# Tiled kv products with a compact mask, and denominators spread over four chunks, in a gated linear-attention and SwiGLU kernel

## Chip, cores, metric

The kernel runs on one core of one Trainium2 chip. The metric is the device time of one execution in microseconds (us); a "span" is the time from the first to the last instruction in a profiled execution. A ratio compares runs of the same rounds alone. Engine names: PE is TensorE, DVE is VectorE, ACT is ScalarE, POOL is GpSimd.

## The reference, cut to what matters

```python
# x: (1, 2048, 512) bf16; 32 heads of 16; F = 1376
pq, pk = phi(q), phi(k)                         # q, k, v from x @ wqkv
kv  = einsum("bhsd,bhse->bhde", pk, v)          # one 16x16 block per head
z   = einsum("bhsd->bhd", pk)
num = einsum("bhqd,bhde->bhqe", pq, kv)
den = einsum("bhqd,bhd->bhq", pq, z)[..., None] + 1e-6
a   = reshape(num / den) @ wo
b   = (silu(x @ w1) * (x @ w3)) @ w2
out = g * a + (1 - g) * b                       # g = sigmoid(x . gate_w)
```

The kernel never forms v. It accumulates XP = x^T pk over all tokens, forms kv from wv and XP once, and folds kv and wo into one matrix W. kv is needed only where row and column belong to the same head, so of each 128x128 product only the 16x16 blocks on its diagonal survive a mask.

## The kernel before

The change touches the passage between the sweep over the keys and the SwiGLU chunks of the first 512 tokens. A "chunk" is 128 of the 1376 hidden features; each has four gate_ps and four up_ps products of 512 columns.

```python
kvT_ps = psX.tile([P, KC, P], FP32, tag="XP0", name="kvT_ps")      # KC = 4, P = 128
for c in range(KC):
    csl = slice(c * P, (c + 1) * P)
    for dc in range(KC):
        nc.tensor.matmul(kvT_ps[:, c, :], lhsT=wv_sb[:, dc, csl], rhs=XP_sb[:, dc, csl],
                         start=(dc == 0), stop=(dc == KC - 1))
nc.vector.tensor_tensor(out=kvT_sb[:], in0=kvT_ps[:],
                        in1=blockmask[:, None, :].to_broadcast([P, KC, P]), op=ALU.mult)
emit_omg(0)                            # om and its reciprocal, 128x4
for fc in range(3):
    if fc == 0:
        emit_ffn(0, fc)
        continue
    emit_den(0, 2 * fc - 2)            # qz on GpSimd, then a reduction on VectorE
    emit_ffn(0, fc, between=lambda: emit_den(0, 2 * fc - 1))
    # ... fc == 1: 16 products W_ps, each 32x32, from kvT_sb[gsl, c, gsl]
    for i in ((2, 3) if fc == 1 else (0, 1)):      # ScalarE: W_ps to W_sb
        nc.scalar.activation(out=W_sb[:, i, :], in_=W_ps[i][:], func=ACT.Copy, scale=2.0)
# ... chunks 3 to 9 without denominators
```

In a chunk (emit_ffn) ScalarE makes th = tanh(gate_ps), VectorE makes gs from th and gate_ps, then whatever "between" holds, then hT from up_ps and gs. gate_ps and up_ps come from a pool of four buffers, so the products of chunk n wait for gs and hT of chunk n-2. Chunks 4 and 6 borrow other buffers (XP0 to XP3). Further names in the lines below: r_ps are the products of the last 96 hidden features and of the gate, and hr their hidden product on GpSimd; qz is the product whose sums over a head are the denominators, and rden their reciprocals, which scale pq; om is the 128x4 factor by whose reciprocal the output is scaled.

## Time and profile before

| | before |
|---|---|
| time, median of 3 | 179.11 us (178.67 to 179.57) |
| span of the profiled run | 176.9 us |
| TensorE busy | 97% |
| VectorE, ScalarE, GpSimd busy | 67%, 37%, 38% |
| last r_ps product to first gate_ps (the kv stage) | 0.977 us |
| lost ahead of gate_ps and up_ps of chunk 3 | 0.38 us |

TensorE sets the time. Its busy share hides small losses, because recorded matmuls overlap (a 512-wide one is recorded as 0.38 us long, and the next starts 0.216 us after it).

### The profile page before, as it was taken

The page shows a single profiled execution, that of the slowest core. Times are in us where ns is not written, and L with a number is a line of the kernel's source. Part 1 is how long each engine was busy: PE and PEld are TensorE (multiplying, and loading weights), DVE is VectorE, ACT ScalarE, POOL GpSimd, SP SyncE. Part 2 cuts the span into 40 slices and gives each one's busy share as a digit, 9 for nine tenths or more (in the row PEclk, how much of TensorE's full clock was granted, in tenths as well). Part 3 has the DMA queues.
Part 4 walks back from the last instruction along what each step waited for, and adds up shares of the span by engine and source line. Part 5 has one row for each costly group of instructions (what it writes and reads, how often), then busy time and mean ns, then how long its engine had stood idle before and what let it go on. Part 6 is the DMA issues. An engine that isn't in the chain of part 4 may idle for free.

```text
span 176.9 us, 2497 instructions
## 1 busy us (share of the span) xinstructions
PE 172.3 (97%) x879; PEld 83.1 (47%) x895; DVE 118.6 (67%) x204; ACT 65.2 (37%) x123; POOL 66.5 (38%) x96
## 2 busy tenths in 40 slices
PE   7999999999999999999999999999999999999994
PEld 3444444474445454444454544444545444444463
DVE  0586858899999737597776375978754669776000
ACT  4524224476333333333243333242433323331222
POOL 6197655789064323272003232820032329100000
PEclk9999999999999999999999999999999999999999
DMA  5999899941004011123000111240002012200012
GB/s 175 229 298 223 247 308 364 352 129 28 9 21 97 7 41 37 37 59 89 0 4 7 38 36 37 60 94 2 0 7 66 12 61 59 65 0 0 30 33 59
DMA packets 30381, 15.14 MB, mean 86 GB/s; under 512 B 20929, under 2 KB 30241, under 8 KB 30369
## 3 DMA queue, kind: packets, MB, share of 16 engines
q1 hardware_dynamic: 29952, 14.67, 30.2%
q10 hardware_dynamic: 416, 0.31, 0.6%
q8 instruction: 7, 0.11, 0.3%
q14 instruction: 6, 0.04, 0.1%
HBM read 8.42 MB, written 2.10 MB: 59 GB/s over the span
## 4 chain that ended last, share of the span: by engine, by line
PE 88%; DVE 5%; POOL 3%; issue 2%; ACT 0%; DVEq 0%; POOLq 0%
PE o_ps L372 19%; PE up_ps L330 18%; PE gate_ps L322 18%; PE o_ps L363 8%; PE q_ps L220 6%; PE XP L207 6%; PE k_ps L187 5%; PE r_ps L244 2%; PE k L187 2%; PE o_ps L367 2%; PE warm L164 2%; POOL pks L197 1%; POOL zt L421 1%; DVE hT L342 1%; DVE phi_m L145 1%
## 5 line engine op out<-in xcount | busy, mean ns | idle before, releaser
L322 PE MATMUL gate_ps<-xT,w_sb 128*128 128x512 bf16 x157 | 40.7, 379 | 0.3
L330 PE MATMUL up_ps<-xT,w_sb 128*128 128x512 bf16 x156 | 40.5, 379 | 0.3 <-DVE hT L342 0.2
L228 POOL TENSOR_TENSOR qz<-pq,z_sb 128x512 f32<-128x512 bf16 x16 | 18.5, 1162 | 57.0 <-DVE pq L148 57.0
L335 ACT ACTIVATE th<-gate_ps 128x512 bf16<-128x512 f32 x40 | 23.9, 598 | 39.6 <-PE gate_ps L322 38.1
L372 PE MATMUL o_ps<-w_sb,hT 128*128 128x512 bf16 (+3 forms) x176 | 37.1, 355 | 0.2
L337 DVE SCALAR_TENSOR_TENSOR gs<-th,gate_ps 128x512 bf16<-128x512 bf16 x40 | 27.3, 682 | 5.4 <-ACT th L335 5.1
L342 DVE TENSOR_TENSOR hT<-up_ps,gs 128x512 bf16<-128x512 f32 x40 | 27.6, 691 | 3.7
L145 DVE TENSOR_SCALAR phi_m<-phi_e 128x512 bf16<-128x512 bf16 x32 | 13.6, 424 | 21.2 <-ACT phi_e L143 21.0
L372 PEld LDWEIGHTS <-hT 128*128 128x128 bf16 x180 | 16.8, 98 | 17.8
L330 PEld LDWEIGHTS <-w_sb 128*128 128x128 bf16 x160 | 15.7, 98 | 19.2 <-issue 0.4
L322 PEld LDWEIGHTS <-w_sb 128*128 128x128 bf16 x160 | 15.5, 98 | 18.7 <-issue 0.4
L297 POOL TENSOR_TENSOR pqn<-pq,rden 128x256 bf16<-128x256 bf16 x32 | 19.0, 626 | 13.8 <-DVE rden L288 13.1
L377 ACT ACTIVATE o_out<-o_ps,omg 128x512 bf16<-128x512 f32 x15 | 10.3, 688 | 28.9 <-PE o_ps L372 26.3
L197 POOL TENSOR_TENSOR pks<-pks,pk_sb 128x512 f32<-128x512 f32 x15 | 17.6, 1174 | 7.3 <-DVE pk_sb L148 6.7
L363 PE MATMUL o_ps<-W_sb,pqT 128*128 128x512 bf16 (+3 forms) x71 | 16.6, 355 | 0.1
L220 PE MATMUL q_ps<-wq_sb,xT 128*128 128x512 bf16 x63 | 16.4, 379 | 0.1
L207 PE MATMUL XP<-pk_sb,x_sb 128*128 128x512 bf16 x62 | 16.2, 379 | 0.1
L231 DVE TENSOR_REDUCE den<-qz 128x32 f32<-128x512 f32 x16 | 10.9, 684 | 7.9 <-POOL qz L228 7.8
L143 ACT ACTIVATE phi_e<-k_ps 128x512 bf16<-128x512 f32 x12 | 7.2, 597 | 14.4 <-PE k_ps L187 13.3
L143 ACT ACTIVATE phi_e<-q_ps 128x512 bf16<-128x512 f32 x16 | 9.6, 597 | 7.8 <-PE q_ps L220 7.8
L187 PE MATMUL k_ps<-wk_sb,xT 128*128 128x512 bf16 x48 | 12.3, 379 | 0.0
L148 DVE SCALAR_TENSOR_TENSOR pq<-q_ps,phi_m 128x512 bf16<-128x512 f32 x16 | 11.1, 691 | 0.5
(60 smaller groups left out, 117.1 us busy)
## 6 DMA issues: line engine op xcount, KB each, us to landing
w_sb<-in_B_w_dram SPq DMA_DIRECT2D x4, 640.0 KB, 7.3
out_dram<-o_out SPq DMA_DIRECT2D x15, 128.0 KB, 1.7
w_sb<-in_B_w_dram SPq DMA_DIRECT2D x1, 1280.0 KB, 12.2
x_sb<-in_A_x_dram SPq DMA_DIRECT2D x2, 512.0 KB, 5.2
x_sb<-in_A_x_dram SPq DMA_DIRECT2D x1, 768.0 KB, 5.1
wq_sb<-in_A_wqkv_dram SPq DMA_DIRECT2D x1, 512.0 KB, 6.4
wv_sb<-in_A_wqkv_dram SPq DMA_DIRECT2D x1, 512.0 KB, 6.4
wo_sb<-in_A_wo_dram SPq DMA_DIRECT2D x1, 512.0 KB, 10.0
```

The source lines that it names most:

```text
L187: nc.tensor.matmul(k_ps[:], lhsT=xT[:, kc, t * P : (t + 1) * P], rhs=wk_sb[:, kc, :], start=(kc == 0), stop=(kc == KC - 1),)
L197: nc.gpsimd.tensor_add(pks[:], pks[:], pk_sb[:, t, :])
L207: nc.tensor.matmul(XP_ps[dc][:], lhsT=x_sb[:, t, dc * P : (dc + 1) * P], rhs=pk_sb[:, t, :], start=(t == 0), stop=(t == NT - 1),)
L220: nc.tensor.matmul(q_ps[:], lhsT=xT[:, kc, ts_tok], rhs=wq_sb[:, kc, :], start=(kc == 0), stop=(kc == KC - 1),)
L297: nc.gpsimd.tensor_tensor(out=pqn[:].rearrange("p (i c e) -> p c i e", i=NG, c=KC)[:, :, :, dsl], in0=st[tb, "pq"][:, tt, :].rearrange("p ...
L322: nc.tensor.matmul(gate_ps[:], lhsT=w1_sb[:, kc, fsl], rhs=xT[:, kc, tok_sl], start=(kc == 0), stop=(kc == KC - 1),)
L330: nc.tensor.matmul(up_ps[:], lhsT=w3_sb[:, kc, fsl], rhs=xT[:, kc, tok_sl], start=(kc == 0), stop=(kc == KC - 1),)
L335: nc.scalar.activation(out=th[:], in_=gate_ps[:], func=ACT.Tanh, scale=0.5)
L337: nc.vector.scalar_tensor_tensor(out=gs[:], in0=th[:], scalar=1.0, in1=gate_ps[:], op0=ALU.add, op1=ALU.mult)
L342: nc.vector.tensor_tensor(out=st[tb, "hT"][:, fc, :], in0=up_ps[:], in1=gs[:], op=ALU.mult)
L363: nc.tensor.matmul(o_ps[:], lhsT=st[tb, "pqT"][:, c, tsl], rhs=W_sb[:, c, a:b], start=(c == 0), stop=False,)
L372: nc.tensor.matmul(o_ps[:], lhsT=st[tb, "hT"][:, fc, tsl], rhs=w2_sb[:, fc, a:b], start=False, stop=(fc == FC - 1),)
```

## The change

It has two parts. The kv products compute only 32x32 diagonal blocks: 64 products of 128x32 with 32 moving columns in four column groups take the place of 16 full ones, and the mask is four times smaller. The four reductions of denominators go one to a chunk into chunks 1 to 4, instead of two each into chunks 1 and 2, and the evictions of W_ps on ScalarE get fixed places between the tanh of those chunks.

```diff
+    diagmask = consts.tile([P, G], FP32, name="diagmask")              # G = 32
+    for i in range(NG):
+        gsl = slice(i * G, (i + 1) * G)
+        nc.gpsimd.tensor_copy(diagmask[gsl, :], blockmask[gsl, gsl])
-    kvT_sb = consts.tile([P, KC, P], BF16, name="kvT_sb")
+    kvT_sb = consts.tile([P, KC, G], BF16, name="kvT_sb")
 ...
-        kvT_ps = psX.tile([P, KC, P], FP32, tag="XP0", name="kvT_ps")
+        kvT_ps = psX.tile([P, KC, G], FP32, tag="XP0", name="kvT_ps")
         for c in range(KC):
-            csl = slice(c * P, (c + 1) * P)
             for dc in range(KC):
-                nc.tensor.matmul(
-                    kvT_ps[:, c, :], lhsT=wv_sb[:, dc, csl], rhs=XP_sb[:, dc, csl],
-                    start=(dc == 0), stop=(dc == KC - 1),
-                )
+                for i in range(NG):
+                    bsl = slice(c * P + i * G, c * P + (i + 1) * G)
+                    nc.tensor.matmul(
+                        kvT_ps[i * G : (i + 1) * G, c, :], lhsT=wv_sb[:, dc, bsl],
+                        rhs=XP_sb[:, dc, bsl], start=(dc == 0), stop=(dc == KC - 1),
+                    )
 ... (mask product on 128x4x32, W_ps from kvT_sb[gsl, c, :])
-        for fc in range(3):
-            ...
-            emit_den(0, 2 * fc - 2)
-            emit_ffn(0, fc, between=lambda: emit_den(0, 2 * fc - 1))
+        emit_ffn(0, 0)
+    with tc.manual_schedule(engines={ENG.DVE, ENG.Activation}):
+        for fc in range(1, TPB + 1):
+            emit_ffn(0, fc, between=lambda: emit_den(0, fc - 1))
+            ... (fc == 1: W_ps as before)
+            for i in {1: (2,), 2: (3, 0), 3: (1,)}.get(fc, ()):
+                emit_W_sb(i)
```

More of the change, by code (lines that the diff above doesn't have):

```diff
@@ L445, with emit_W_sb @@
         )
-        kvT_ps = psX.tile([P, KC, P], FP32, tag="XP0", name="kvT_ps")
+        kvT_ps = psX.tile([P, KC, G], FP32, tag="XP0", name="kvT_ps")
         for c in range(KC):
-            csl = slice(c * P, (c + 1) * P)
             for dc in range(KC):
-                nc.tensor.matmul(
-                    kvT_ps[:, c, :], lhsT=wv_sb[:, dc, csl], rhs=XP_sb[:, dc, csl],
-                    start=(dc == 0), stop=(dc == KC - 1),
-                )
+                for i in range(NG):
[4 more added lines that the diff above has]
+                    )
         nc.vector.tensor_tensor(
             out=kvT_sb[:], in0=kvT_ps[:],
-            in1=blockmask[:, None, :].to_broadcast([P, KC, P]), op=ALU.mult,
+            in1=diagmask[:, None, :].to_broadcast([P, KC, G]), op=ALU.mult,
         )
         emit_omg(0)
-        for fc in range(3):
-            if fc == 0:
-                emit_ffn(0, fc)
-                continue
-            emit_den(0, 2 * fc - 2)
-            emit_ffn(0, fc, between=lambda: emit_den(0, 2 * fc - 1))
+        emit_ffn(0, 0)
+    with tc.manual_schedule(engines={ENG.DVE, ENG.Activation}):
+        W_ps = [psX.tile([P, D], FP32, tag=f"XP{i}", name=f"W_ps{i}") for i in range(NG)]
+        def emit_W_sb(i):
+            nc.scalar.activation(out=W_sb[:, i, :], in_=W_ps[i][:], func=ACT.Copy, scale=2.0)
+        for fc in range(1, TPB + 1):
+            emit_ffn(0, fc, between=lambda: emit_den(0, fc - 1))
             if fc == 1:
-                W_ps = [psX.tile([P, D], FP32, tag=f"XP{i}", name=f"W_ps{i}") for i in range(NG)]
                 for i in range(NG):
@@ L471 @@
                         nc.tensor.matmul(
-                            W_ps[i][c * G : (c + 1) * G, :], lhsT=kvT_sb[gsl, c, gsl],
+                            W_ps[i][c * G : (c + 1) * G, :], lhsT=kvT_sb[gsl, c, :],
                             rhs=wo_sb[gsl, c, :], start=True, stop=True,
                         )
-            for i in ((2, 3) if fc == 1 else (0, 1)):
-                nc.scalar.activation(out=W_sb[:, i, :], in_=W_ps[i][:], func=ACT.Copy, scale=2.0)
-    for fc in range(3, FC):
+            for i in {1: (2,), 2: (3, 0), 3: (1,)}.get(fc, ()):
+                emit_W_sb(i)
+    for fc in range(TPB + 1, FC):
         emit_ffn(0, fc)
```

## The prediction

> **What bounds the kernel now.** I read the page first, for the bound.
>
> ```profile
> PE 172.3 (97%) x879; PEld 83.1 (47%) x895; DVE 118.6 (67%) x204; ACT 65.2 (37%) x123; POOL 66.5 (38%) x96
> ...
> PE 88%; DVE 5%; POOL 3%; issue 2%; ACT 0%; DVEq 0%; POOLq 0%
> ```
>
> TensorE (PE) is busy for 97% of the 176.9 us span and makes up 88% of the chain that ended last. So the change is worth what it takes out of TensorE's stream, or puts into it, and nothing else. The list of waits of TensorE has only two entries, and one of them lies in the stage that the change touches:
>
> ```profile
> PE up_ps L330 <- DVE hT L342: 0.2, 1, 0.2
> ```
>
> A busy TensorE can hide more than that, because the recorded end of a matmul overlaps the next one's start. I therefore read starts, not busy time, in the timeline of TensorE from the kv products (L450) on. Columns: start us, us until the last one's recorded end, engine, line.
>
> ```profile
> 37.04 1.06 PE L450 MATMUL kvT_ps<-XP_sb,wv_sb 128*128 128x128 bf16 x16
> 37.93 1.03 PE L322 MATMUL gate_ps<-xT,w_sb 128*128 128x512 bf16 x4
> ...
> 40.52 1.03 PE L330 MATMUL up_ps<-xT,w_sb 128*128 128x512 bf16 x4
> 41.48 0.43 PE L471 MATMUL W_ps<-wo_sb,kvT_sb 32*32 32x512 bf16 x16
> 41.85 1.04 PE L322 MATMUL gate_ps<-xT,w_sb 128*128 128x512 bf16 x4
> 42.72 1.03 PE L330 MATMUL up_ps<-xT,w_sb 128*128 128x512 bf16 x4
> 43.63 1.02 PE L322 MATMUL gate_ps<-xT,w_sb 128*128 128x512 bf16 x4
> 44.83 1.02 PE L330 MATMUL up_ps<-xT,w_sb 128*128 128x512 bf16 x4 [0.17 <-DVE hT L342]
> 45.69 1.03 PE L322 MATMUL gate_ps<-xT,w_sb 128*128 128x512 bf16 x4
> ```
>
> Where nothing waits, a group of four starts 0.863 us after the one before it (44.83 to 45.69), so one 512-wide matmul takes 0.216. From 42.72 to 43.63 is 0.91, that is 0.05 too much; from 43.63 to 44.83 is 1.20, 0.34 too much. The **loss is 0.39 us**, though the wait shows 0.17. Its cause is seen on VectorE (DVE) and GpSimd (POOL):
>
> ```profile
> 39.21 0.65 DVE L454 TENSOR_TENSOR kvT_sb<-kvT_ps,blockmask 128x512 bf16<-128x512 f32 x1
> 39.78 1.03 DVE L275 TENSOR_SCALAR om<-el 128x4 f32<-128x4 f32 x1
> ...
> 40.94 0.66 DVE L337 SCALAR_TENSOR_TENSOR gs<-th,gate_ps 128x512 bf16<-128x512 bf16 x1
> ...
> 44.09 0.68 DVE L342 TENSOR_TENSOR hT<-up_ps,gs 128x512 bf16<-128x512 f32 x1
> ```
>
> ```profile
> 39.62 4.61 POOL L228 TENSOR_TENSOR qz<-pq,z_sb 128x512 f32<-128x512 bf16 x4
> ```
>
> VectorE runs without a pause here and is late: the first gs waited for nothing but VectorE's own queue (its tanh ended at 39.60). Before it stand the kv mask of 0.65 us, and a 128x4 operation of 1.03 us under a running qz. Then chunks 1 and 2 each put two reductions of denominators beside gs and hT: four operations some 0.60 us apart, 2.4 us, against TensorE's 1.73 us a chunk. So the hT of chunk 1 starts at 44.09, and up_ps of chunk 3, which needs its buffer (four in the pool, two a chunk), starts at 44.83. On ScalarE (ACT) four evictions of W_ps stand together:
>
> ```profile
> 41.93 2.06 ACT L476 ACTIVATE W_sb<-W_ps 128x512 bf16<-128x512 f32 x4 [0.61 <-PE W_ps L471]
> 43.85 0.63 ACT L335 ACTIVATE th<-gate_ps 128x512 bf16<-128x512 f32 x1
> ```
>
> The tanh of chunk 2 starts at 43.85, although its gate_ps was done at 42.89: 0.96 us late. This is hidden today, because VectorE reaches the gs of chunk 2 only at 45.28, but it would show once VectorE is quick.
>
> [...]the 16 W_ps products: they start within 0.05 us, so 0.0034 us apart. [...]No kv-like case, the same tile reloaded again and again, is in this trace; nearest is the 64-wide tail of the last output:
>
> ```profile
> 173.79 0.46 PE L372 MATMUL o_ps<-w_sb,hT 128*128 128x64 bf16 x10
> ```
>
> Taking 0.19 for the last one's own duration (the single L367 matmul of that width shows 0.19), nine steps take 0.27 us: 30 ns for a pair of load and matmul. [...]The matmul before it is this one:
>
> ```profile
> 41.17 0.38 PE L330 MATMUL up_ps<-xT,w_sb 128*128 128x512 bf16 x1
> ```
>
> Its stream ends at 41.17 + 0.22 = 41.39, and W_ps starts at 41.48: 0.09 us. The last W_ps product starts at 41.53 and streams until 41.75, the next gate_ps starts at 41.85: 0.10 us. So one visit to a tiled mode costs **0.19 us**. [...]om (L275) of 128x4 takes 1.03 us under qz, while in its three other executions, later in the span, it takes 0.16 us.
>
> **The change, part by part.** (a) kv products. Removed: 16 matmuls of 128 columns, 0.89 us (37.04 to 37.93). Added: 64 of 32 columns, each with a load of 32 columns, in four column groups; the moving columns fall from 16 x 128 = 2048 to 64 x 32 = 2048 if groups ran one after the other, and to 512 if four run at once. If the four of a round overlap,[...] about 30 ns: 16 x 0.030 = 0.48, plus 0.19 for the mode: 0.67 us, so -0.22 us. This is an estimate, from the tail's pair[...]. If they don't overlap,[...] 2.0 us, +1.1 us. I take the first as likelier (55%), because W_ps shows pairs following at 0.0034 us in distinct tiles, column neighbours among them. With 30% for the second and the rest between, the weighted cost is about +0.2 us.
> (b) The mask: 128x128 instead of 128x512 elements. The rden product of 128x128 (L288) takes 0.28 us, so VectorE gains 0.4 us. It is not at the end of a path itself: kvT_sb is ready at 39.86 today and needed at 41.48. Its side effect: om could start at about 39.42, before qz starts at 39.62, and finish in 0.16 us; then a further 0.9 us of VectorE is saved. That is a race of 40 ns and I give it half.
> (c) Denominators: chunks 1 to 4 carry three VectorE operations each, 3 x 0.60 = 1.80 us against 1.73: a drift of 0.07 a chunk, absorbed. Working it out without the luck of (b): gs(0) stays at 40.9, then in steps of 0.60 hT(0) 41.5, gs(1) 42.1, den(0) 42.7, hT(1) 43.3 to 44.0; up_ps of chunk 3 wants its buffer at 44.5. So the whole **0.39 us** goes. The four qz (1.16 us each, the last done at 44.23) come before their reductions.
> (d) ScalarE in fixed order: tanh, then one, two and one evictions of 0.60 us; gate_ps of chunk 2 is evaluated at about 42.9 instead of 43.85. XP2 and XP3 come free before 45, and chunk 4 wants them at 45.35 without the loss. No time of its own, but it makes (c) safe.
> (e) rden is about 1.5 us later, as the fourth reduction moves from chunk 2 to 4. The first pqT (its products start at 50.22 today, its transfer takes 2.3) is wanted at 57.79: 4 us of slack hide it. The four GpSimd copies for the compact mask fit in its idle 3.95 us before 7.66.
> Sum: -0.39 (c) + 0.2 (a, weighted) = about -0.2 us; with the likelier branch of (a) alone -0.6. I write -0.3: 179.11 - 0.3 = **178.8 us**.
>
> **Rivals.** *Serial column groups*: kv takes 2.0 us, +1.1 - 0.39 = +0.7, 179.8 us. [...]Against it: the 0.0034 us of W_ps. *The sequencer becomes the bound*: 128 instructions instead of 32. The trace shows nothing slower than 30 ns for a pair when short; if 64 pairs cost that each, the result is the serial one again. *The loss moves*: a wait of the same size returns at chunk 4 or 6, where buffers XP0 to XP3 are borrowed, or at the first output block through the later rden; then (c) is worth 0 and the time is 179.1 - 0.2 to 180.2. The slacks in (d) and (e) speak against it.
>
> **Range and chances.** The likelier branch gives 178.5, the serial one 179.8, and the three runs of before spread from 178.67 to 179.57. I set 178.1 to 179.8. All branches lie within 1% while 2% is 3.6 us, so same 0.97, faster 0.02, slower 0.01.
>
> **What would show it.** In the timeline after: from the first kv product to gate_ps of chunk 0, 0.67 us if the groups overlap, 2.0 if not; steps of 0.863 from gate_ps of chunk 2 to chunk 4; no wait on hT; kvT_sb at 0.28 us; om at 0.16 or 1.0 us; tanh of chunk 2 within 0.1 us of its gate_ps. The prediction is wrong if kv takes over 2.2 us, if a gap over 0.3 us opens before chunk 8 or at the first output block, or if the stages that the diff doesn't touch change.

The sum came to -0.39 (c) + 0.2 (a, weighted) = about -0.2 us, to -0.6 with the likelier branch of (a), and -0.3 was written. The time of a product behind the serial branch's 2.0 us was the author's estimate without a measurement (with the tail's 30 ns it would be 64 x 0.030 + 0.19 = 2.1 us). Why a round should take 30 ns was not shown. The matmul "before it" is the one before W_ps; the 0.19 us are the 0.09 and 0.10 read around W_ps. Why om is slow under qz was not shown either; what stands is that it took 1.03 us there and 0.16 elsewhere.

## The result

The changed kernel took 178.26 us (median of 6, 177.97 to 178.57), the kernel before 179.27 us (median of 6, 178.61 to 179.57). The ratio is 0.995 with a 95% interval of 0.9926 to 0.9974. A ratio here is the mean time of one kernel's fast runs over that of the other's in the same rounds, so it is not quite the ratio of the quoted medians.

The page of the kernel after, the same two lines:

```profile
PE 173.1 (98%) x943; PEld 83.3 (47%) x943; DVE 117.6 (67%) x204; ACT 65.4 (37%) x123; POOL 67.1 (38%) x100
...
PE 98%; DVE 0%; issue 0%
```

The chain that ended last is now TensorE almost alone, where VectorE and GpSimd had 8% of it. In TensorE's list of waits the one for hT is gone; only that of the warm-up at the start is left:

```profile
PE warm L168 <- PEq L521: 0.8, 1, 0.8
```

The timeline of TensorE in the kernel after (start us, us to the last recorded end, engine, line):

```profile
35.94 1.50 PE L248 MATMUL r_ps<-wr_sb,xT 128*128 128x193 bf16 x16
37.37 0.66 PE L455 MATMUL kvT_ps<-XP_sb,wv_sb 128*32 128x32 bf16 x64
37.96 1.04 PE L326 MATMUL gate_ps<-xT,w_sb 128*128 128x512 bf16 x4
...
41.89 1.04 PE L326 MATMUL gate_ps<-xT,w_sb 128*128 128x512 bf16 x4
42.76 1.03 PE L334 MATMUL up_ps<-xT,w_sb 128*128 128x512 bf16 x4
43.62 1.03 PE L326 MATMUL gate_ps<-xT,w_sb 128*128 128x512 bf16 x4
44.49 1.03 PE L334 MATMUL up_ps<-xT,w_sb 128*128 128x512 bf16 x4
```

From 42.76 on the groups start 0.86 to 0.87 us apart: the 0.38 us of before are gone. The last r_ps product starts at 37.19, so the kv stage takes 37.96 - 37.19 = 0.77 us, against 0.98.

On VectorE and GpSimd of the kernel after:

```profile
39.44 0.25 DVE L459 TENSOR_TENSOR kvT_sb<-kvT_ps,diagmask 128x128 bf16<-128x128 f32 x1
39.62 0.31 DVE L279 TENSOR_SCALAR om<-el 128x4 f32<-128x4 f32 x1
39.96 0.18 DVE L283 RECIPROCAL omg<-om 128x4 f32<-128x4 f32 x1
40.06 0.66 DVE L341 SCALAR_TENSOR_TENSOR gs<-th,gate_ps 128x512 bf16<-128x512 bf16 x1
...
42.62 0.69 DVE L346 TENSOR_TENSOR hT<-up_ps,gs 128x512 bf16<-128x512 f32 x1
```

```profile
38.85 1.05 POOL L261 TENSOR_TENSOR hr<-upr,gsr 128x192 bf16<-128x192 f32 x2
39.87 4.53 POOL L232 TENSOR_TENSOR qz<-pq,z_sb 128x512 f32<-128x512 bf16 x4
```

The mask takes 0.25 us and om 0.31 instead of 1.03: om now ends at 39.93, 0.02 after the last hr, where it used to end (40.81) 0.02 after the first qz. The hT of chunk 1 starts at 42.62 and ends 1.18 us before up_ps of chunk 3 starts. On ScalarE the tanh of chunk 2 comes right after its gate_ps, between evictions:

```profile
42.03 0.60 ACT L471 ACTIVATE W_sb<-W_ps 128x512 bf16<-128x512 f32 x1 [0.67 <-PE W_ps L479]
42.96 0.60 ACT L339 ACTIVATE th<-gate_ps 128x512 bf16<-128x512 f32 x1 [0.33 <-PE gate_ps L326]
```

**Why spans are not compared directly.** The spans are 176.9 and 176.5 us, 0.3 us apart unrounded (176.85 and 176.53). But the first XP product starts at 8.08 us in one trace and at 8.32 in the other:

```profile
8.08 1.03 PE L207 MATMUL XP<-pk_sb,x_sb 128*128 128x512 bf16 x4
```

```profile
8.32 1.03 PE L211 MATMUL XP<-pk_sb,x_sb 128*128 128x512 bf16 x4
```

From that product to the end it is 168.77 us before and 168.21 after: **0.56 us less**, namely 0.21 in the kv stage and 0.37 to 0.38 from the wait, within 0.03 us. In the traces the first XP product starts anywhere from 7.95 to 9.20 us, while "XP to end" repeats to 0.01 us for the same work. So I judge every experiment by XP to end, and the timed runs only say how much of it survives the scatter of the start.

### The profile page after: what moved, and what is told of

Same layout as the page of the kernel before. It is cut to its first block, busy times and chain, and to the rows that moved or that the text cites. A ratio compares the mean times of both kernels' runs of the same rounds, so it can differ in the third digit from the quotient of the medians.

```text
span 176.5 us, 2613 instructions
## 1 busy us (share of the span) xinstructions
PE 173.1 (98%) x943; PEld 83.3 (47%) x943; DVE 117.6 (67%) x204; ACT 65.4 (37%) x123; POOL 67.1 (38%) x100
## 4 chain that ended last, share of the span: by engine, by line
PE 98%; DVE 0%; issue 0%
PE gate_ps L326 20%; PE o_ps L376 20%; PE up_ps L334 20%; PE o_ps L367 8%; PE XP L211 8%; PE q_ps L224 8%; PE k_ps L191 6%; PE r_ps L248 3%; PE k L191 2%; PE o_ps L371 2%; PE warm L168 2%; PE xTp L181 0%; PE kvT_ps L455 0%; PE W_ps L479 0%; DVE o_last L385 0%
## 5 line engine op out<-in xcount | busy, mean ns | idle before, releaser
L334 PE MATMUL up_ps<-xT,w_sb 128*128 128x512 bf16 x160 | 41.1, 379 | 0.0
```

What stands on the lines that cost most here:

```text
L334: nc.tensor.matmul(up_ps[:], lhsT=w3_sb[:, kc, fsl], rhs=xT[:, kc, tok_sl], start=(kc == 0), stop=(kc == KC - 1),)
```

## The experiments

The four questions: does the time agree with the traces' 0.56 us; which part removes the wait; what is the ScalarE order worth; and what paces the kv stage. "Stage" is from the last r_ps product to the first gate_ps; "lost" is the sum of gaps over the normal step between gate_ps and up_ps groups from chunk 2 on. The single runs had no repetition, so only their traces count.

| run | stage us | lost us | XP to end us | ratio (95%) |
|---|---|---|---|---|
| before | 0.977 | 0.38 | 168.77 | |
| after | 0.770 | 0 | 168.21 | 0.995 (0.9926 to 0.9974) |
| after_again | 0.770 | 0 | 168.21 | 0.9987 (0.9964 to 1.0009) |
| kv_only | 0.772 | 0 | 168.21 | 0.9959 (0.9938 to 0.9981) |
| den_only | 0.976 | 0 | 168.40 | 0.9982 (0.9962 to 1.0001) |
| om_early | 0.977 | 0 | 168.41 | 0.9991 (0.9969 to 1.0013) |
| mask_copies_only | 0.976 | 0.37 | 168.77 | 1.0012 (0.999 to 1.0035) |
| den_only_act_free | 0.977 | 0.27 | 168.68 | single run |
| act_free | 0.771 | 0.26 | 168.47 | single run |
| kv_only_plus2 | 0.770 | 0.90 | 169.11 | single run |
| after_plus2 | 0.771 | 0.28 (0.05 more at chunk 9) | 168.54 | single run |
| groups_serial | 0.874 | 0 | 168.32 | single run |
| kv_twice | 1.305 | 0 | 168.82 | single run |
| one_group_extra | 2.355 | 0 | 169.80 | single run |

### The whole change again (after_again)

No edit.

> The whole change again, for a narrower interval, because the first measurement (178.26 against 179.27 us, 1.0 us less) gave more than the two traces show: from the first XP product to the end 168.22 us against 168.77, that is 0.56 us less (kv stage 0.21, the wait for hT 0.39, small change elsewhere). If only the stage counts, the ratio comes out near 1 - 0.56/179.2 = 0.9969, so about 178.6 us beside 179.2. If something at the start of the program changes too, the ratio stays at 0.995, and XP starts earlier than in the kernel before.

Measured: 178.76 us (median of 6) beside 179.12 (median of 11). XP to end is again 168.21 us. The interval of the first rounds (0.9926 to 0.9974) and of these (0.9964 to 1.0009) both hold 0.9969, which is 1 - 0.56/179.2. So the 1.0 us of the first medians was in part luck, and the traces' 0.56 us is the size that all results agree with. Of the start: XP began at 8.79 us here, later than before, so nothing in the start got faster.

### The kv part alone (kv_only)

```diff
 (kernel before, plus: diagmask, the 64 tiled products, the 128x4x32 mask)
 (denominators and ScalarE order as before)
```

> Only the tiled kv products with the compact mask; denominators (two in each of chunks 1 and 2) and ScalarE order as before. By the steps of the prediction (the wait goes by spreading the denominators) this saves the kv stage alone, 0.21 us, and the gap of 0.34 us before up_ps of chunk 3 stays. Rival, from the trace after: the smaller mask lets om finish[...] (om 0.31 instead of 1.03 us, gs of chunk 0 at 40.06 instead of 40.94), so VectorE is 0.9 us earlier and the hT of chunk 1 ends at about 43.9, before 44.5: then the gap goes with the denominators untouched and this kernel saves the full 0.58 us.

Two lines of TensorE's timeline:

```profile
43.82 1.03 PE L326 MATMUL gate_ps<-xT,w_sb 128*128 128x512 bf16 x4
44.68 1.03 PE L334 MATMUL up_ps<-xT,w_sb 128*128 128x512 bf16 x4
```

They are gate_ps and up_ps of chunk 3, 0.86 us apart: no gap. XP to end is 168.21 us, the same as with the whole change. **The rival won**: with om at 0.31 us and a small mask, VectorE reaches the hT of chunk 1 in time although chunks 1 and 2 still carry two denominators each. In this kernel the spreading adds nothing to the time.

### The denominators alone (den_only), and om moved alone (om_early)

```diff
 den_only: (kernel before, plus: denominators one to a chunk, fixed ScalarE order)

 om_early:
+        emit_omg(0)
         nc.vector.tensor_tensor(out=kvT_sb[:], in0=kvT_ps[:], ...)
-        emit_omg(0)
```

> Only the spread denominators with the fixed ScalarE order; kv products in full width and mask as before. The prediction: om still about 1.0 us under qz, gs of chunk 0 near 40.9, hT of chunk 1 at 43.3 to 44.0, no wait of TensorE, 0.39 us saved, kv stage 0.89 us as before. Rival (om alone decides): the gap stays at 0.3 us and nothing is saved.

> The kernel before with one pair of VectorE operations moved: om and its reciprocal stand ahead of the kv mask instead of after it, so they start at about 39.3, before the first qz (39.62). Nothing else is changed. If the [...]om is the root of the wait, om falls to 0.16 us, gs of chunk 0 starts near 40.1, and the 0.39 us of TensorE goes, with kv stage and denominators as they were. If four operations a chunk are the root, a gap of over 0.2 us before up_ps of chunk 3 stays.

Both remove the whole gap: 168.40 and 168.41 us, 0.37 and 0.36 less than before, with the kv stage unchanged. (The timed runs alone would not show so little: both intervals hold 1.) The lines of om (durations: shortest, median, longest of four), first in den_only, then in om_early:

```profile
L275 DVE TENSOR_SCALAR om<-el x4: 158/159/1024, 40.0 to 139.3; 128x4 f32<-128x4 f32 x4
```

```profile
L275 DVE TENSOR_SCALAR om<-el x4: 158/159/482, 39.5 to 139.5; 128x4 f32<-128x4 f32 x4
```

Moving two small instructions by one place is worth as much as the whole rearrangement of denominators. My figure for om_early was off in one point: om took 0.48 us, not 0.16; it now started under hr instead of qz and ended at 40.01, and gs of chunk 0 started at 2.45 us after gate_ps instead of 3.01. In 13 of the 14 traces om ends 0.02 to 0.03 us after the GpSimd operation that was running when it started, whether that was qz (40.81 beside 40.79 in the kernel before) or hr (39.93 beside 39.90 in the kernel after). The exception is one_group_extra below: there om started 0.05 us before the end of hr and 6 ns before the first qz, and took its 0.16 us.

### How much slack each part buys (kv_only_plus2, after_plus2)

```diff
-        nc.vector.tensor_reduce(out=den..., in_=qz...)
+        for _ in range(3 if (tb, tt) == (0, 0) else 1):
+            nc.vector.tensor_reduce(out=den..., in_=qz...)
```

> The kv part alone, with the first denominators' reduction written three times instead of once (same result), so that VectorE carries two more operations of 0.60 us before the hT of chunk 1. The slack account: in kv_only that hT ends 5.92 us after the first gate_ps, up_ps of chunk 3 would start at 6.53, so there is 0.6 us of slack; with 1.2 us more it ends at 7.12 and TensorE should lose 0.6 to 0.7 us. XP to end 168.8 to 168.9 us.

> The whole change with the same two extra reductions. Here the hT of chunk 1 ended at 5.34, 1.19 us of slack; with 1.2 us more it ends at 6.54 and TensorE should lose 0.0 to 0.1 us. XP to end 168.2 to 168.3 us. If both extra-work kernels lose the same, the spreading of the denominators bought no slack.

The two waits in TensorE's list for kv_only_plus2:

```profile
PE gate_ps L327 <- DVE gs L342: 0.4, 1, 0.4
PE up_ps L335 <- DVE hT L347: 0.2, 1, 0.2
```

The gap came back: 0.90 us in kv_only_plus2 and 0.28 in after_plus2. Both are larger than I had written, because the three reductions of one tile took 2.12 us, 0.71 each and not 0.60, and the hT of chunk 1 moved by 1.4 us, not 1.2. With the measured end of hT the account agrees to 0.01 us. Without a wait up_ps of chunk 3 starts 6.53 us after the first gate_ps (44.49 - 37.96 in the kernel after); with a wait it starts some 0.06 us after the end of hT (6.84 to 6.90 in the kernel before):

| run | hT of chunk 1 ends, us after first gate_ps | end + 0.06 - 6.53 | lost, measured |
|---|---|---|---|
| before | 6.84 | 0.37 | 0.38 |
| om_early | 6.30 | none | 0 |
| den_only | 6.23 | none | 0 |
| kv_only | 5.92 | none | 0 |
| after | 5.35 | none | 0 |
| after_plus2 | 6.75 | 0.28 | 0.28 |
| kv_only_plus2 | 7.37 | 0.90 | 0.90 |

So the spreading buys 0.6 us more slack in either pair (5.92 to 5.35, 7.37 to 6.75), which only shows when something else makes VectorE late. A single trace gives this slack only roughly: in after_again, the same kernel as after, the same hT ended at 5.60.

### The order on ScalarE (act_free, den_only_act_free)

```diff
-    with tc.manual_schedule(engines={ENG.DVE, ENG.Activation}):
+    with tc.manual_schedule(engines={ENG.DVE}):
```

> The kernel after without the fixed ScalarE order: the scheduler puts the four evictions of W_ps together again, ahead of the tanh of chunk 2. Prediction, step d: the late tanh would show once VectorE is quick. Rival, from the trace of the run with the kv part alone, where the tanh of chunk 2 came 5.93 us after the first gate_ps (4.99 us with the fixed order) and no gap followed: chunks 4 and 6 borrow other buffers, so after up_ps of chunk 3 nothing needs VectorE's results soon. Then TensorE shows no gap and XP to end stays at 168.21 us.

TensorE and VectorE in act_free:

```profile
53.62 1.03 PE L334 MATMUL up_ps<-xT,w_sb 128*128 128x512 bf16 x4
54.75 0.59 PE L326 MATMUL gate_ps<-xT,w_sb 128*128 128x512 bf16 x2
```

```profile
45.06 0.69 DVE L341 SCALAR_TENSOR_TENSOR gs<-th,gate_ps 128x512 bf16<-128x512 bf16 x1 [1.26 <-ACT th L339]
```

The rival that I had put beside my step d fell. VectorE stood for 1.26 us before gs of chunk 2, and then carried the denominators of chunks 2 to 4 and the three rden operations, so it stayed late. No gap opened at chunk 3, but some ten microseconds later, at gate_ps of chunk 9, the step is 1.13 instead of 0.86 us: 0.26 us lost. The list of waits of this run does not show it.

> The spread denominators alone, on full-width kv products, and with the ScalarE order left to the scheduler. The run of the whole change without the fixed order lost 0.26 us at gate_ps of chunk 9, because VectorE waited 1.26 us for the tanh of chunk 2 and then carried denominators and the reciprocal. The same loss should appear here: no gap before up_ps of chunk 3, 0.2 to 0.4 us before gate_ps of chunk 9, XP to end 168.6 to 168.8 us, so that most of what the spreading won is lost again. Rival: the late tanh costs nothing, 168.40 us as in the run with the fixed order.

The same loss, 0.27 us at gate_ps of chunk 9, XP to end 168.68 us. So with the denominators spread, the fixed ScalarE order is what keeps the gain; without it three quarters of 0.37 us go again. In kv_only the scheduler's order had the same late tanh (5.93 us after gate_ps) and cost nothing, because there the denominators were done by chunk 2. The same account as above shows it: gate_ps of chunk 9 needs the buffer that gs of chunk 7 frees, and without a wait it starts 16.02 us after the first gate_ps. That gs ends at 15.43 us in kv_only and 15.27 in after, but at 16.23 in act_free: 16.23 + 0.06 - 16.02 makes 0.27 us, where 0.26 was measured.

### What paces the kv stage (groups_serial, kv_twice, one_group_extra)

```diff
 groups_serial:
-            for dc in range(KC):
-                for i in range(NG):
+            for i in range(NG):
+                for dc in range(KC):

 kv_twice:
-        for c in range(KC):
+        for c in [c for _ in range(2) for c in range(KC)]:

 one_group_extra: (after the 64 products, four passes over c and dc with i = 0 only)
```

> The kernel after, with the two inner loops of the kv products exchanged: four products in a row now go to the same column group, before the next group comes. Same 64 products, same loads. If overlap of the four groups makes the kv stage short (my step a), the stage grows towards the serial figure of the prediction:[...] 1.6 to 2.0 us from the last r_ps product to the first gate_ps instead of 0.77. If only the number of instructions counts (the second half of the stage ran at 8.3 ns a pair whichever group), it stays near 0.8.

> The kernel after with all 64 kv products issued twice over the same four column groups (the second pass starts afresh, so the result is the same). In the trace after, the first 32 products came in rounds of four every 25 ns (6.2 ns a product), the rest 8.3 ns apart. If that second pace is what the stage settles at[...], the 64 more cost 64 x 8.3 ns = 0.53 us (stage from the last r_ps product to gate_ps 1.30 us). If a round[...], 25 to 30 ns as in the prediction, is the limit: 0.40 to 0.48 us.

> The kernel after with 64 further kv products, all into column group 0 (repeats of that group's own products, so the result is the same). This measures one group reloaded and used again and again, with nothing beside it. My prediction's figure for that[...] would make it 1.6 to 1.8 us more. The exchanged loops, where the first products of one group started 13 ns apart, suggest 64 x 13 ns = 0.8 us more. If the pace of issue alone counts, 0.53 us as in the kernel with all groups twice.

TensorE in one_group_extra:

```profile
38.25 2.25 PE L458 MATMUL kvT_ps<-XP_sb,wv_sb 128*32 128x32 bf16 x128
40.43 0.82 PE L326 MATMUL gate_ps<-xT,w_sb 128*128 128x512 bf16 x2
```

and in kv_twice:

```profile
37.84 1.20 PE L455 MATMUL kvT_ps<-XP_sb,wv_sb 128*32 128x32 bf16 x128
38.97 1.04 PE L326 MATMUL gate_ps<-xT,w_sb 128*128 128x512 bf16 x3
```

64 more products over four groups cost 1.305 - 0.770 = 0.535 us, 8.4 ns each; 64 more in one group cost 2.355 - 0.770 = 1.585 us, 24.8 ns each (their starts in the trace are 25 ns apart). So a product with a new load takes 24.8 ns in one column group, and over four groups a third of that, 8.4 ns. The finer picture is in the starts of the products: in the kernel after the first 32 come in rounds of four, 1 to 5 ns from one to the next within a round and 25 ns from round to round; from then on they come 8.3 ns apart, 33 ns a round. The 25 ns of a round is what one group alone took for a product (24.8); the rest goes at a slower pace, nearly that of the 64 more in kv_twice (8.4). Why the pace changes after 32 products no run tested, so the cause of 8.3 ns stays open.

Exchanging the loops cost 0.10 us, not the 0.8 to 1.2 that I expected if order mattered: 63 steps took 0.59 us, 9.3 ns each, far from the 24.8 of one group alone. So with four products in a row for one group the groups still overlapped. The trace does not tell the groups apart, so how is left open.

### Do the mask's copies slow the start? (mask_copies_only)

```diff
 (kernel before, plus the four lines that fill diagmask, unused)
```

> The kernel before with nothing added but the four GpSimd copies that make the compact mask (unused here). The question is whether they slow the start. In the nine traces that have them so far, the first XP product starts at 8.12 to 9.20 us (mean 8.65), in the four without at 8.01 to 8.41 (mean 8.20). If the copies cause this, the ratio to the kernel before is about 1 + 0.45/179.1 = 1.0025 and XP starts after 8.4. If it is chance, the ratio is 1.000 within its interval of some 0.002, as the timed runs so far suggest (the kernels with the copies were faster than before by 0.1 to 0.5%). From XP to the end it must show 168.77 us either way, with the gap before up_ps of chunk 3.

XP started at 7.95 us, the earliest of all traces, and the ratio is 1.0012 (0.999 to 1.0035), so the interval holds both 1.000 and 1.0025. The later starts in the other traces with these copies look like chance, but the timed runs alone do not exclude a quarter of a per cent. XP to end is 168.77 us with the gap, as expected.

No version that beats the changed kernel came out of this: by XP to end kv_only equals it with a smaller edit, and no wait is left in the stage.

## Why the prediction was right

The measured 178.26 us lies in the range of 178.1 to 179.8; the forecast of 178.8 was 0.5 us too high beside it. Part of that is scatter: the repeat gave 178.76, beside 179.12 for the kernel before. What the traces support is -0.56 us, against -0.3 forecast. Step by step:

- *The loss of 0.39 us ahead of chunk 3 is real and goes.* Right: den_only, which only spreads the denominators and fixes the ScalarE order, gains 0.37 us.
- *Its cause* I gave as VectorE's queue: mask, an om of 1.03 us, two denominators a chunk. Right as a list. Wrong, or at least incomplete, in the working: I credited the removal to (c) alone, and said of (b) that it saves VectorE time without being on a path. kv_only shows that (a) with (b) removes the same wait alone, and om_early that 0.5 us less of om is enough. The parts do not add: kv part 0.56 us, denominators 0.37, both 0.56.
- *(a) The kv stage.* The likelier branch was 0.67 us where before had 0.89, -0.22. The stage, on the same terms (from the end of the last r_ps stream, 37.19 + 0.08, to gate_ps at 37.96), took 0.69 us, -0.21. The two gaps where the tile of the products changes, from 128\*128 to 128\*32 and back, predicted at 0.19 us in sum from W_ps, measured 0.09 at the entry (37.28 to 37.37) and 0.10 at the exit (37.86 to 37.96). The 64 products between took 0.48 us as predicted. That is luck: a round took 25 ns at first and 33 later, not 30 all along. And the 30 ns came from another case: the tail's pairs load 128 columns and stream 64, and 64 alone take 0.027 us, an estimate from the 0.216 us of 512.
- *Where the size was off.* The term mis-sized is the weight of 30% on the serial branch and the rest between, which turned -0.22 into +0.2 and the sum of about -0.6 into -0.2; from there to the -0.3 written no step leads. (With the middle of the two branches for "the rest" the weights give nearer +0.3.) The range also stops at 179.8, though its own rival "the loss moves" reached 180.2. The trace's -0.56 us is the likelier branch almost to the digit. The serial branch did have a true core: one group alone costs 24.8 ns a product (one_group_extra), so at that pace the 64 would have taken 1.6 us, an estimate from this number.
- *(b) The race of om* was given half. om escaped qz but not hr: 0.31 us, between the two figures. The one clean win, 0.16 us, is in one_group_extra, whose longer kv stage delays om.
- *(d) The ScalarE order* has no time of its own but makes (c) safe: right, act_free and den_only_act_free lose 0.26 and 0.27 us without it, though at chunk 9 and not at chunk 4, where the prediction looked. The tanh of chunk 2 started 0.03 us after the recorded end of its gate_ps.
- *(e) The later rden* costs nothing: right, no gap follows in the first output block, though the first pqT products start 1.9 us later (52.12 instead of 50.22), not 1.5.
- *The rivals* "serial", "sequencer" and "the loss moves" did not come true in the kernel after, though two of them show when provoked: a pace of 8.3 ns a product over the second half of the stage (that the sequencer sets it was not shown), and a loss that moves to chunk 9 when ScalarE is left free.

## What to carry to other kernels

When an engine that is not the bound makes the bound wait, count the slack at the one instruction that waits, as in the table of hT ends; then remedies that look independent turn out to compete for the same fraction of a microsecond, and the cheapest is enough. Look for small operations that are long only while another engine works: here om took 1.03 us under qz and 0.16 later in the span, and moving this 128x4 operation by one place did the work of a rearranged schedule. Judge changes of half a microsecond by a stretch of the trace that repeats to a hundredth, not by medians whose start alone scatters by one.
